# Each of the first 22 loads asked for only when the fourth load ahead of it has landed

## The chip, the cores and the metric

One core of a Trainium2 chip runs the kernel. The metric is device microseconds of one execution; a kernel's time is the median of its runs. TensorE was granted its full clock (1.0) throughout the profiled execution.

## What is computed

Linear attention with a quadratic feature map, and behind it a feed-forward layer on all 4352 tokens, in fp32:

```python
def phi(x):                       # r = 8: 64 features from 32 channels
    a = np.einsum('rd,bhsd->bhsr', S1, x)
    b = np.einsum('rd,bhsd->bhsr', S2, x)
    return np.einsum('bhsi,bhsj->bhsij', a, b).reshape(*x.shape[:-1], r * r)
q_p, k_p = phi(q), phi(k)         # batch 4, heads 4, 1088 positions
kv, z = einsum('bhsf,bhsd->bhfd', k_p, v), k_p.sum(2)
x = einsum('bhsf,bhfd->bhsd', q_p, kv) / (einsum('bhsf,bhf->bhs', q_p, z) + 1e-6)
h = x @ w_in                      # 4352 x 128 by 128 x 2048
out = (h * clip(h + 3, 0, 6) / 6) @ w_out
```

## The kernel before, in words

Tokens lie in the free dimension, channels on the partitions. The 4352 tokens are cut into eight chunks of 512 and one of 256 (`CHUNKS`); the 2048 hidden units into eight pairs of 128. For each chunk and pair TensorE makes `h` in three passes (high part of x by high and low part of the weights, low part of x by the high part), ACT and DVE make the gate, ACT and POOL or DVE split it into `gh` and `gl`, and TensorE adds it up into `o`.

The inputs arrive by DMA, all of it asked for by SyncE (SP). The keys come in eight groups (`k0` to `k7`, 256 or 320 KB), the values likewise (`v0` to `v7`, 264 or 330 KB), the queries by chunk (`q0` to `q8`, 256 KB), the two weight matrices in nine blocks (`wi0` and `wi1` with 256 KB, `wi2` to `wi4` and `wo0` to `wo3` with 512 KB). A weight block arrives as 64-bit words in a buffer `raw` and is turned into fp32 and split in two by seven steps: `scale` (L337) and `rest` (L340) on ACT, `sign` (L343) and `shift` (L347) on DVE, `word` (L351) on POOL, `high` (L354) on ACT, `low` (L357) on POOL or DVE.

The order of everything is written out by hand in `ORDER`, a list of names; each engine runs its own steps in that order. Each load is a step `ld_...` of SP (L322), put in by `load`, and has no needs but a free buffer. The loads stand in `ORDER` as k0, wi0, k1, wi1, q0, v0, v1, wi2, wo1, q1, k3, k2, wi3, v2, k5, v3, wi4, wo0, q3, q2, k4, wo2; before wo2, and only there, SP has another step to do, `move_1` (eight DMAs, L602). A small DMA of the projections (`sb_raw`, 80 KB, L288) goes ahead of them all and is not one of the loads that `load` makes.

What reads the early loads: `mm_k0` reads k0 (TensorE, L375), `scale_wi0` and `rest_wi0` read wi0, `rest_wi1` and `sign_wi1` read wi1, `mm_q0` reads q0, `kvt_0_...` (L405) read v0 and v1 together with the features of k0 and k1 (L385), `rest_wi2`, `sign_wi2` and `scale_wi2` read wi2. On ACT `rest_wi2` stands just ahead of `twice_0` (L439, L440), which copies out the sums of the first keys, and `scale_wi2` just behind it. On DVE `spread` (L427) and `shift_wi2` follow each other.

```python
def emit(_):
    nc.sync.dma_start(view(at(b)), place(name))

return plan.add(f"ld_{name}", SP, [], emit, [b]), b
```

Of the kernel before, what the change touches and what calls it, by code (L numbers as in the profile page):

```python
# [50 lines left out]
FAR = ((1,), (2, 3), (4, 5), (6, 7), (8,))  # L51

HALVED = 1
FIRST = 2


# [177 lines left out]
def fused_kernel(ctx: ExitStack, tc: tile.TileContext, inputs, places, outT):  # L234
    nc = tc.nc
# [17 lines left out]
    def at(buf):  # L253
        return room[buf.tag][buf.slot]
# [20 lines left out]
    def place(name):  # L275
        source, i, j = places[name]
        return inputs[source][i:j].rearrange("(p x) -> p x", p=P)
# [37 lines left out]
    s_done = plan.add("s_tr", PE, [s_done], s_tr, [st])  # L315
    s_done = plan.add("s_back", ACT, [s_done], s_back, [st])

    def load(tag, name, view):
        b = Buf((tag,))

        def emit(_):
            nc.sync.dma_start(view(at(b)), place(name))  # L322

        return plan.add(f"ld_{name}", SP, [], emit, [b]), b

# [2 lines left out]
    def weights(nm, hi, lo, j):  # L328
        name = f"{nm}{j}"
        i, k = BLOCKS[nm][j : j + 2]  # L330
        n = k - i
        hi, lo = hi[:, i:k], lo[:, i:k]
        ld, raw = load("raw", name, lambda t: t[:, :n])
        wb, rb, sb_ = Buf(("w",)), Buf(("r",)), Buf(ANY)

# [62 lines left out]
    def keys(b):  # L398
# [11 lines left out]
        for g in (2 * b, 2 * b + 1):  # L410
            t0, n = KGROUPS[g]
            lk, kb = load("kT", f"k{g}", lambda t, n=n: t[:, : n * P])
            lv, vb = load("v", f"v{g}", lambda t, n=n: t[:, :n, :].rearrange("p t x -> p (t x)"))
            parts, ab, ph = features(f"k{g}", n, "kph", lk, kb, ANY if b == 0 else ("a",), KEY_COLS[b])
            for t in range(n):
                i = t0 + t - b * KT
                prevs = plan.add(f"kvt_{b}_{i}", PE, [parts[t], lv, prevs], partial(kvt, n=n, t=t, i=i, ab=ab, ph=ph, val=vb), [ph, vb, sums, ab])
# [196 lines left out]
    def step(c, fp):  # L614
        c0, n = CHUNKS[c]
        hb, gb, gh, gl = (Buf((t,)) for t in ("h", "g", "gh", "gl"))
        ji, jo = (max(j for j, i in enumerate(BLOCKS[nm]) if i <= fp * 2 * P) for nm in ("wi", "wo"))
        halved = c < HALVED and fp < FIRST
        done = [None, None]
# [141 lines left out]
```

## Time and profile before

| what | us |
|---|---|
| median of 3 runs (228.47 to 229.22) | 228.91 |
| the profiled execution: its own time | 227.95 |
| span of the profiled execution, first to last instruction | 226.2 |
| TensorE busy | 219.7 (97% of the span) |
| ACT, DVE, POOL busy | 165.9, 163.1, 153.7 |

The profiled execution took 1.75 us more than its span, and 0.96 us less than the median. Times in the rows are counted from the first instruction. SP only issues DMAs; a row of SP's timeline is the time that the issue takes, and the DMA lands later by what the issue view gives.

### The profile page before, as it was taken

The numbers are of one execution on the slowest core, as the hardware profiler recorded it, in microseconds if no ns is written. First come the engines' busy times: TensorE is split into PE (matmuls) and PEld (weight loads), VectorE is DVE, ScalarE is ACT, GpSimd is POOL, SyncE is SP. The second block draws the span as 40 slices with busy tenths as digits, with TensorE's granted clock in tenths as the row PEclk, the third lists the DMA queues.
The fourth block names the chain that finished last, engine by engine and source line by source line (L and its number), as shares of the span: only waits on it lengthen the run. The fifth ranks groups of instructions, "written<-read, shape, count | busy, mean of one in ns | idle before, by whom it ended". The sixth has DMA issues, their size and how long they took to land.

```text
span 226.2 us, 4762 instructions
## 1 busy us (share of the span) xinstructions
PE 219.7 (97%) x1888; PEld 174.9 (77%) x1888; DVE 163.1 (72%) x216; ACT 165.9 (73%) x231; POOL 153.7 (68%) x111
## 2 busy tenths in 40 slices
PE   8789999999999999999999999999999999999994
PEld 3568768877788788777887888788888788888993
DVE  2799999999949889677866865686378644648561
ACT  4687997989785878656687865876686777785781
POOL 3859998998199734993899797356640498564471
PEclk9999999999999999999999999999999999999999
DMA  6997149233600001233001113020010000020010
GB/s 206 395 412 281 48 118 380 82 83 78 193 3 0 3 0 47 50 81 130 0 1 48 49 46 93 25 71 0 0 46 3 0 0 0 3 93 0 0 51 23
DMA packets 9430, 17.77 MB, mean 79 GB/s; under 512 B 1728, under 2 KB 2368, under 8 KB 9408
## 3 DMA queue, kind: packets, MB, share of 16 engines
q1 hardware_dynamic: 9408, 17.46, 23.2%
q8 instruction: 15, 0.25, 0.5%
q14 instruction: 7, 0.06, 0.1%
HBM read 11.30 MB, written 2.23 MB: 60 GB/s over the span
## 4 chain that ended last, share of the span: by engine, by line
PE 87%; DVE 5%; POOL 3%; DMA 1%; ACT 1%; issue 0%; SPq 0%; DVEq 0%
PE o L664 41%; PE h L627 14%; PE h L631 13%; PE h L628 13%; PE a L547 2%; DMA raw<-weights_dram 1%; DVE kph L385 1%; PE o L405 1%; PE a L542 1%; POOL gl L647 1%; DVE o L343 1%; POOL w L351 1%; DVE w L347 1%; PE a L375 1%; POOL wi_lo L357 1%; POOL kph L385 0%
## 5 line engine op out<-in xcount | busy, mean ns | idle before, releaser
L647 POOL TENSOR_TENSOR gl<-g,gh 128x1024 fp32r<-128x1024 f32 (+1 forms) x45 | 106.3, 2372 | 56.7 <-ACT gh L644 38.4
L641 DVE SCALAR_TENSOR_TENSOR g<-g,h 128x1024 f32<-128x1024 f32 (+1 forms) x72 | 82.8, 1153 | 35.4 <-ACT g L638 35.2
L638 ACT ACTIVATE g<-h 128x1024 f32<-128x1024 f32 (+1 forms) x72 | 70.7, 982 | 35.3 <-PE h L631 20.7
L644 ACT CAST gh<-g 128x1024 fp32r<-128x1024 f32 (+1 forms) x72 | 70.2, 1002 | 11.0 <-DVE g L641 6.0
L627 PE MATMUL h<-xh,wi_hi 128*128 128x512 f32 (+1 forms) x148 | 56.2, 381 | 0.0
L628 PE MATMUL h<-xh,wi_lo 128*128 128x512 f32 (+1 forms) x148 | 55.1, 373 | 0.0
L664 PE MATMUL o<-gh,wo_hi 128*128 128x512 f32 (+1 forms) x144 | 54.2, 379 | 0.0
L664 PE MATMUL o<-gh,wo_lo 128*128 128x512 f32 (+1 forms) x144 | 54.0, 378 | 0.0
L631 PE MATMUL h<-xh,wi_hi 128*128 128x512 f32 (+1 forms) x148 | 49.9, 374 | 0.0
L664 PE MATMUL o<-gl,wo_hi 128*128 128x512 f32 (+1 forms) x144 | 41.3, 380 | 0.1
L647 DVE TENSOR_TENSOR gl<-g,gh 128x1024 fp32r<-128x1024 f32 (+1 forms) x27 | 33.1, 1235 | 5.9 <-PE o L664 3.6
L627 PEld LDWEIGHTS h<-xh,wi_hi 128*128 128x128 f32 x148 | 27.8, 188 | 7.5 <-DVE g L641 1.2
L631 PEld LDWEIGHTS h<-xh,wi_hi 128*128 128x128 f32 x148 | 27.7, 188 | 5.5 <-DVE xh L470 0.2
L628 PEld LDWEIGHTS h<-xh,wi_lo 128*128 128x128 f32 x148 | 27.8, 188 | 4.6
L664 PEld LDWEIGHTS o<-gh,wo_hi 128*128 128x128 f32 x144 | 27.1, 188 | 5.3 <-issue 0.4
L664 PEld LDWEIGHTS o<-gh,wo_lo 128*128 128x128 f32 x144 | 27.1, 188 | 4.9
L664 PEld LDWEIGHTS o<-gl,wo_hi 128*128 128x128 f32 x144 | 26.0, 188 | 5.5 <-POOL gl L647 0.5
L590 POOL TENSOR_TENSOR qph<-ab 128x512 f32<-128x512 f32 (+1 forms) x16 | 16.1, 1018 | 0.2
L351 POOL TENSOR_TENSOR w<-w,r 128x512 int32<-128x512 int32 (+1 forms) x9 | 10.4, 1166 | 2.5 <-DVE w L347 2.0
L597 DVE STREAM_TRANSPOSE raw<-qph 128x512 f32<-128x512 f32 (+1 forms) x16 | 10.4, 665 | 1.9 <-POOL qph L590 1.9
L385 DVE TENSOR_TENSOR kph<-a,ab 128x512 f32<-128x512 f32 (+1 forms) x14 | 8.8, 635 | 0.5 <-ACT ab L378 0.5
L405 PE MATMUL o<-kph,v 128*32 128x64 f32 x288 | 6.2, 223 | 1.1 <-DVE kph L385 1.0
(104 smaller groups left out, 160.1 us busy)
## 6 DMA issues: line engine op xcount, KB each, us to landing
raw<-weights_dram SPq DMA_DIRECT2D x7, 512.0 KB, 6.3
phT<-raw SPq DMA_DIRECT2D x56, 64.0 KB, 2.0
qT<-tokens_dram SPq DMA_DIRECT2D x8, 256.0 KB, 6.0
outT_dram<-os SPq DMA_DIRECT2D x8, 256.0 KB, 2.2
v<-tokens_dram SPq DMA_DIRECT2D x4, 330.0 KB, 4.8
kT<-tokens_dram SPq DMA_DIRECT2D x4, 320.0 KB, 5.7
v<-tokens_dram SPq DMA_DIRECT2D x4, 264.0 KB, 6.1
kT<-tokens_dram SPq DMA_DIRECT2D x4, 256.0 KB, 5.7
```

What stands on the lines that cost most here:

```text
L351: nc.gpsimd.tensor_tensor(w, w, at(rb)[:, :n], op=ALU.add)
L385: engines[e].tensor_tensor(out, a_, b_, op=ALU.mult)
L590: engines[e].tensor_tensor(out, a_, b_, op=ALU.mult)
L597: nc.vector.transpose(turned_view()[:, :, r * half : (r + 1) * half].rearrange("p f (t w) -> p t f w", w=Q), src)
L627: nc.tensor.matmul(at(hb)[:, u, i:k], wi_hi[:, f], x, start=True, stop=False)
L628: nc.tensor.matmul(at(hb)[:, u, i:k], wi_lo[:, f], x, start=False, stop=False)
L631: nc.tensor.matmul(at(hb)[:, u, i:k], wi_hi[:, f], at(x_buf[c])[:, 1, i:k], start=False, stop=True)
L638: nc.scalar.activation(at(gb)[:, :, :n], at(hb)[:, :, :n], AF.Relu, bias=3.0, scale=1.0)
L641: nc.vector.scalar_tensor_tensor(at(gb)[:, :, :n], at(gb)[:, :, :n], 6.0, at(hb)[:, :, :n], op0=ALU.min, op1=ALU.mult)
L644: nc.scalar.copy(at(gh)[:, :, :n], at(gb)[:, :, :n])
L647: engines[e].tensor_tensor(at(gl)[:, :, :n], at(gb)[:, :, :n], at(gh)[:, :, :n].bitcast(F32), op=ALU.subtract)
L664: nc.tensor.matmul(at(ob)[:, :n], w, x[:, :n], start=left == acc["all"] and i == 0, stop=left == 1 and i == len(pairs) - 1)
```

## The change

Each call of `load`'s `emit` is kept in a list in the order in which SP issues them. From the fifth to the 22nd load an edge is added that makes the load wait for the landing of the load that stands four places ahead. The order of operations is as it was.

```diff
+AHEAD = 4
+FIRST_LOADS = 22
...
+    first = []
+
     def load(tag, name, view):
         b = Buf((tag,))
 
         def emit(_):
-            nc.sync.dma_start(view(at(b)), place(name))
+            i = nc.sync.dma_start(view(at(b)), place(name))
+            if AHEAD <= len(first) < FIRST_LOADS:
+                in_line = mybir.DependencyInfo(mybir.DependencyClass.Sync, mybir.DependencyReason.DATA)
+                tc.add_manual_dep(i.ins, first[-AHEAD].ins.name, in_line, reason="loads in line")
+            first.append(i)
```

## Rows read from the trace of the kernel before

**Rows 1.** The page's 40 slices of 5.655 us: TensorE's busy tenths, the DMA rate.

```profile
PE   8789999999999999999999999999999999999994
...
GB/s 206 395 412 281 48 118 380 82 83 78 193 3 0 3 0 47 50 81 130 0 1 48 49 46 93 25 71 0 0 46 3 0 0 0 3 93 0 0 51 23
```

**Rows 2.** Windows view, one stretch: its length, busy us by engine, clock, DMA.

```profile
17.40:226.00 208.60, 205.44 (x1596) 165.96 (x1589) 151.68 (x190) 154.29 (x201) 143.77 (x90) 1.00 0.18 57
```

**Rows 3.** Chain that ended last, up to 24 us: start, us, what.

```profile
1.64 3.09 DMA raw<-weights_dram
...
11.90 0.69 DVE w L347
```

**Rows 4.** SP's timeline: start, us, what is issued, count.

```profile
1.18 0.42 SPq L322 DMA_DIRECT2D kT<-tokens_dram  x1
...
2.59 0.43 SPq L322 DMA_DIRECT2D raw<-weights_dram  x1
3.06 0.43 SPq L322 DMA_DIRECT2D qT<-tokens_dram  x1
3.54 0.91 SPq L322 DMA_DIRECT2D v<-tokens_dram  x2
4.49 0.92 SPq L322 DMA_DIRECT2D raw<-weights_dram  x2
...
7.38 0.33 SPq L322 DMA_DIRECT2D raw<-weights_dram  x1
8.01 0.33 SPq L322 DMA_DIRECT2D v<-tokens_dram  x1
...
24.73 6.29 SPq L602 DMA_DIRECT2D phT<-raw  x8
```

**Rows 5.** Issue view, one issue each (sb k0 wi1 q0 v0 wi2 wi3 wo2 v6): KB, us to landing.

```profile
sb_raw<-weights_dram SPq DMA_DIRECT2D x1, 80.0 KB, 1.9
...
kT<-tokens_dram SPq DMA_DIRECT2D x1, 256.0 KB, 2.6
...
raw<-weights_dram SPq DMA_DIRECT2D x1, 256.0 KB, 4.1
...
qT<-tokens_dram SPq DMA_DIRECT2D x1, 256.0 KB, 4.2
...
v<-tokens_dram SPq DMA_DIRECT2D x1, 264.0 KB, 4.5
...
raw<-weights_dram SPq DMA_DIRECT2D x1, 512.0 KB, 5.6
...
raw<-weights_dram SPq DMA_DIRECT2D x1, 512.0 KB, 8.5
...
raw<-weights_dram SPq DMA_DIRECT2D x1, 512.0 KB, 3.7
...
v<-tokens_dram SPq DMA_DIRECT2D x1, 330.0 KB, 3.1
```

**Rows 6.** ACT's timeline: readers of wi1, wi2 and wi3; twice_0; in brackets idle before.

```profile
6.67 0.43 ACT L340 ACTIVATE r<-raw 128x256 int32<-128x256 uint32 x1 [0.72 <-DMA raw<-weights_dram]
...
10.19 0.70 ACT L340 ACTIVATE r<-raw 128x512 int32<-128x512 uint32 x1 [0.58 <-DMA raw<-weights_dram]
10.90 0.27 ACT L439 COPY kvt<-o 128x128 f32<-128x128 f32 x1
...
11.14 0.69 ACT L337 ACTIVATE w<-raw 128x512 f32<-128x512 f32 x1
...
17.86 0.68 ACT L337 ACTIVATE w<-raw 128x512 f32<-128x512 f32 x1
```

**Rows 7.** DVE's timeline: features of k1 and k0, spread, shift_wi2.

```profile
8.58 1.29 DVE L385 TENSOR_TENSOR kph<-a,ab 128x512 f32<-128x512 f32 x2 [0.50 <-ACT ab L378]
...
11.57 0.41 DVE L427 TENSOR_TENSOR z_diag<-mask,o 128x256 f32<-128x256 f32 x1
11.90 0.68 DVE L347 SCALAR_TENSOR_TENSOR w<-w,o 128x512 uint32<-128x512 uint32 x1
```

## The prediction, as made before the result was known

> **What bounds the kernel now.** I read the page's slices first. They fall into two parts [rows 1]: in the first three slices, up to 17 us, TensorE is not quite full and the DMAs run at about 400 GB/s (395 and 412 in the second and third slice); behind them TensorE is full to the last slice. The windows view says the same in one row: from 17.4 us to the end TensorE is busy 205.44 of 208.60 us [rows 2], and a bound of that kind cannot be moved by loads. So the change can act only on when this full stretch begins: what comes later there comes later at the end, one for one, since no idle time stands behind it in which to catch up.
>
> Next the chain of waits, for the first 24 us only [rows 3]. It holds one load, wi0 (asked for at 1.64, 3.09 us to landing). From there on it is engine work: ACT and POOL, then DVE from the features of k1 at 8.58 [rows 7] through `shift_wi2` at 11.90 to the low part of x, whereupon the full stretch of matmuls starts. No second load stands in it.
>
> Then SP's timeline and the issue view together, which give the landings (issue plus time to landing) [rows 4, 5]: k0 1.18 + 2.6 = 3.8; wi1 2.59 + 4.1 = 6.7; q0 3.06 + 4.2 = 7.3; v0 3.54 + 4.5 = 8.0; wi2 4.49 + 5.6 = 10.1; wi3 7.38 + 8.5 = 15.9. The same size takes the longer the later it is asked for: 256 KB take 2.6 us in an empty queue and 4.2 in a full one, and 512 KB rise from 5.6 to 8.5. That is a queue being drained at a steady rate, not a queue that lacks requests. The engines' timelines give who waits for a landing: ACT for wi1 (0.72 us, to 6.67) and for wi2 (0.58 us, to 10.19) [rows 6].
>
> **The change, part by part.** It adds 18 waits, one on each of the loads q0 to wo2, and removes or moves nothing.
>
> The instruction itself costs nothing that counts. SP already waits for landings: v2, the eighth DMA behind v0, is issued at 8.01, just as v0 has landed (8.0), and the issue takes 0.33 us [rows 4, 5]. I read this as a distance of eight that is in force already, and as the price of a wait: the issue follows the landing within hundredths of a microsecond. Behind a waiting load on SP stand only further loads until `move_1` at 24.73 [rows 4]; by then all of them are issued (below), so neither the moves nor the stores feel it.
>
> What counts is whether the transfer engines run dry between a landing and the first bytes of the load that was waiting for it. At that landing three loads are still in the queue. The smallest such three among the loads that something soon waits for are wi1, q0 and v0: 256 + 256 + 264 = 776 KB, which at the 400 GB/s of [rows 1] is 2.0 us of work. Against this stands the round trip, the part of the time to landing that is not transfer. For sb, in an empty queue, it is 1.9 us less 80 KB at 400 GB/s (0.2), so 1.7; for k0 2.6 - 0.65 = 1.95; for v6 3.1 - 0.85 = 2.3; for wo2 3.7 - 1.3 = 2.4 [rows 5]. The last three began in an idle queue, and wo2 and v6 beside the moves' DMAs, so they hold a slow start that a running queue need not show. The cover is 2.0 to 3 us, the round trip 1.7 to 2.4: just covered, or short by a few tenths now and then.
>
> The Trainium skill ("DMA: Bandwidth & Descriptors", section "Anatomy of one DMA") speaks against a wait of this kind: a DMA has a fixed cost of about 2.0 us, most of it receipt of the write, that no deeper work hides once one waits for its end, plus bytes over 436 GB/s. That figure is for the other issue path; with it wi2 would land 2.0 + 1.2 us after its issue at 6.67, at 9.9, before it lands now, and the sum would be zero. The rows give up to half a microsecond more, so their upper end is the harsher.
>
> Now load by load, taking for each the later of two times: its place in the queue as now, or its issue plus the time of its size in an empty queue [rows 5]. The first four, k0 to wi1, are issued as now, so wi0, the only load in the chain, lands where it did. q0 is asked for at 3.82 instead of 3.06 and could land at 3.82 + 2.6 = 6.4, before the 7.3 that its place gives: no change. v0 is asked for when wi0 lands, at 4.75, and with at most the 3.1 of v6 is there by 7.9, before its 8.0. v1 is asked for when k1 lands, which is before wi1 does (6.65), so it is there by 9.75 at the very latest; its matmuls also need features that DVE finishes at 8.58 + 1.29 = 9.87 [rows 7]. wi2 is the first that can slip: it is asked for when wi1 lands, 6.65, so at 6.67, and with 3.7 lands at 10.37 against 10.1, +0.27. With the 1.7 of sb plus 1.3 of transfer it would be 9.7, so its place decides and the slip is nothing.
>
> What would a late wi2 cost? ACT is idle before its first reader at 10.19, so that reader is late by the whole slip; `twice_0` at 10.90 and `scale_wi2` at 11.14 follow it back to back [rows 6], and `shift_wi2` on DVE, which is in the chain, needs the latter's end at 11.83 and starts at 11.90, as soon as `spread` lets it [rows 7]. The room is 0.1 us at most. So a slip of 0.27 puts at most 0.27 us on the end.
>
> The loads behind wi2 are hidden. wi3 lands at 15.9 and its first reader runs at 17.86 [rows 4 to 6]: 2 us of room, and the loads after it have more. Running the same rule on with the empty-queue times, the slip grows from 0.27 to about 0.5 at wi4, and the last load ahead of the moves, k4, is asked for at about 20, 4 us before `move_1`.
>
> Sum: between 0 and +0.27 us on the profiled 227.95. I take 0, since the full queue is nearer to a load that never meets an idle engine than to wo2 and v6, which did. Nothing below zero goes into the sum: the features at 8.58 waited 0.50 us for ACT's copy and not for a load, and an earlier wi2 finds DVE taken, since `spread` ends (11.57 + 0.41) only as `shift_wi2` starts [rows 7]. The median stands 0.96 us above the profiled execution; the change of 0 is put on the median.
>
> **The rivals.**
>
> *The round trip is not covered (slower).* The place is the landing of wi1 at 6.7 and the queue behind it. If each transfer engine that runs dry restarts as slowly as at the very beginning, a load costs more than the empty-queue times, say 0.5 us more: wi2 then lands at 10.87, ACT, `twice_0` and DVE shift by 0.77 less the 0.1 of room, and the time is 228.91 + 0.7 = 229.6. It decides from a landing of wi2 later than 10.2, and is over 0.3% (0.69 us, about what a measurement of this kernel can tell from no change) from 10.9 on. For it: the small gap between cover and round trip. Against it: three loads are in the queue at each landing, and the empty-queue times already contain one slow start.
>
> *Fewer transfers at a time land sooner (faster).* wi0 took 3.09 us where k0 took 2.6 for the same 256 KB [rows 3, 5]; if wi0 had lost these 0.5 us to the loads issued behind it, the chain would start 0.5 us sooner: 228.4. Against it: three of the loads behind it stay as they are, q0's bytes come after those of wi1, and the steady growth of the landing times says that the loads are served in turn. The Trainium skill ("DMA: Bandwidth & Descriptors", section "Latency and other measured facts") has a rule on its side, that a lighter load on HBM makes the fixed cost smaller; no row here shows it.
>
> *The change does nothing.* Both instructions are SP's, and an edge between two instructions of one queue could be taken as kept by their order, without a wait. q0 would be issued at 3.06 as now; the time is 228.9.
>
> **How the numbers follow.** The forecast (waits in force, wi2 late by 0 to 0.27): 0.79, 228.9, its own range 228.6 to 229.3 with the scatter of the runs. No wait: 0.08, 228.9. Round trip not covered: 0.08, 229.2 to 229.8, of which 0.05 lies over 0.3%. Sooner landings: 0.05, 228.1 to 228.5, of which 0.03 lies over 0.3%. So faster 0.03, same 0.92, slower 0.05. The range takes in the half microsecond that the faster rival gives and most of the slower one's: 228.4 to 229.5.
>
> **What would show it.** In the profile after, SP's timeline should have q0 issued at about 3.8, v0 at 4.75, wi2 at 6.7, and k4 near 19.5; the issue view should give times to landing of some 3 to 5 us instead of up to 8.5; ACT's reader of wi2 should start between 10.2 and 10.5, and the full stretch of TensorE at 17.4 to 17.7. The prediction is wrong if wi2's reader starts past 10.9, if wi0 lands before 4.3, or if `move_1` is issued later than now by more than the rest of the chain.

## The result, and the profile after

The changed kernel takes 230.6 us, the median of 11 runs (229.17 to 232.29); the kernel before takes 228.81 us in 11 runs on the same chips (227.99 to 229.23). The ratio is 1.009 with a 95% interval of 1.0061 to 1.0118: slower by 1.8 us. It lies outside the range and on the side that was given 0.05. The runs also differ in something that the profile before did not show: the granted clock of TensorE, averaged over the run, is 1.0 in two of the 11 runs (229.17 and 229.46 us), 0.993 in three (229.67 to 230.60) and 0.982 to 0.985 in six (230.23 to 232.29). Three runs of the kernels below (232.26 us with wi2 alone, 276.31 with distance five, 436.8 with three matmuls fewer) took over 1.5% longer than the fastest of their kernel and count neither in the ratios nor in the counts by clock.

The profiled execution of the changed kernel took 229.46 us with a span of 227.7 us, and is one of the two at full clock. It is 1.5 us longer than the profiled execution of before. The slices that answer to [rows 1] (TensorE's busy tenths, DMA rate):

```profile
PE   8869999999999999999999999999999999999994
...
GB/s 200 292 326 308 182 103 375 122 53 89 202 11 0 3 0 33 63 67 143 0 1 31 65 35 104 20 75 0 0 46 3 0 0 0 3 92 0 0 49 25
```

The rate in the second and third slice is 292 and 326 GB/s where it was 395 and 412, and the first loads go on into the fifth slice. The windows view shows the same in stretches of 2 us (length, busy us of PE, PEld, DVE, ACT and POOL with counts, granted clock, busy share of the DMA engines, GB/s), first before, then after:

```profile
6.00:8.00 2.00, 1.74 (x38) 1.27 (x37) 1.26 (x3) 0.94 (x3) 1.75 (x2) 1.00 1.05 394
8.00:10.00 2.00, 0.88 (x46) 0.76 (x48) 1.50 (x4) 1.22 (x4) 1.84 (x4) 1.00 1.03 416
10.00:12.00 2.00, 1.73 (x63) 1.40 (x63) 2.00 (x5) 1.80 (x5) 1.04 (x2) 1.00 1.03 400
```

```profile
6.00:8.00 2.00, 2.00 (x26) 0.99 (x26) 0.75 (x2) 0.90 (x4) 1.75 (x2) 1.00 0.84 282
8.00:10.00 2.00, 1.35 (x56) 1.15 (x56) 1.88 (x4) 1.24 (x4) 1.32 (x3) 1.00 0.97 318
10.00:12.00 2.00, 1.47 (x54) 1.18 (x54) 1.62 (x4) 0.38 (x2) 1.55 (x3) 1.00 0.92 279
...
19.00:227.50 208.50, 205.43 (x1593) 165.96 (x1589) 151.56 (x190) 154.31 (x201) 143.54 (x90) 1.00 0.19 60
```

The busy share of the DMA engines falls from 1.03 to 1.05 to as little as 0.84, although three or four loads are under way: that fits engines of which some have nothing to do at times. The last row answers to [rows 2]: the full stretch of TensorE is as dense as before (205.43 of 208.50 us), only it begins and ends 1.5 us later.

SP's timeline shows that the waits are in force (start, us, what is issued, count); it answers to [rows 4]:

```profile
2.58 0.43 SPq L328 DMA_DIRECT2D raw<-weights_dram  x1
3.85 0.33 SPq L328 DMA_DIRECT2D qT<-tokens_dram  x1
4.53 2.35 SPq L328 DMA_DIRECT2D v<-tokens_dram  x2
7.24 0.88 SPq L328 DMA_DIRECT2D raw<-weights_dram  x2
...
23.69 0.33 SPq L328 DMA_DIRECT2D kT<-tokens_dram  x1
26.30 0.59 SPq L612 DMA_DIRECT2D phT<-raw  x1
```

q0 is issued at 3.85 (forecast 3.8), v0 at 4.53, wi2 at 7.24 (6.7), k4 at 23.69 (19.5). The issue view for k1, wi1, v1, wi2 and wo1 (KB, us to landing) answers to [rows 5]:

```profile
kT<-tokens_dram SPq DMA_DIRECT2D x1, 320.0 KB, 4.4
...
raw<-weights_dram SPq DMA_DIRECT2D x1, 256.0 KB, 4.6
...
v<-tokens_dram SPq DMA_DIRECT2D x1, 330.0 KB, 3.5
...
raw<-weights_dram SPq DMA_DIRECT2D x1, 512.0 KB, 4.4
...
raw<-weights_dram SPq DMA_DIRECT2D x1, 512.0 KB, 5.6
```

wi2 lands at 7.24 + 4.4 = 11.65 instead of 10.10. ACT's timeline (in brackets idle before) shows what that does to its reader, to `twice_0` and to `scale_wi2`, which answers to [rows 6]:

```profile
11.74 0.67 ACT L350 ACTIVATE r<-raw 128x512 int32<-128x512 uint32 x1 [1.62 <-DMA raw<-weights_dram]
12.30 0.26 ACT L449 COPY kvt<-o 128x128 f32<-128x128 f32 x1
...
12.53 0.70 ACT L347 ACTIVATE w<-raw 128x512 f32<-128x512 f32 x1
```

The reader starts at 11.74 instead of 10.19, 1.55 us later, and the span is 1.5 us longer: one for one. The chain (start, us, what) now goes through two loads, wi1 and wi2, where [rows 3] had only wi0:

```profile
2.58 4.58 DMA raw<-weights_dram
...
7.24 4.41 DMA raw<-weights_dram
```

So between these two profiles the loss is the late landing of wi2. Whether the rest, up to the median, comes with the clock is tested below.

### The profile page after: what moved, and what is told of

It reads as the page before. It is cut to its first block, busy times and chain, and to the rows that moved or that the text cites. A ratio compares the mean times of both kernels' runs of the same rounds, so it can differ in the third digit from the quotient of the medians.

```text
span 227.7 us, 4762 instructions
## 1 busy us (share of the span) xinstructions
PE 220.9 (97%) x1888; PEld 175.5 (77%) x1888; DVE 163.5 (72%) x216; ACT 165.8 (73%) x231; POOL 153.7 (68%) x111
## 4 chain that ended last, share of the span: by engine, by line
PE 91%; DMA 4%; ACT 2%; SPq 1%; issue 1%; ACTq 0%
PE o L674 41%; PE h L637 15%; PE h L641 14%; PE h L638 14%; DMA raw<-weights_dram 4%; PE a L557 2%; PE o L415 2%; PE a L385 2%; PE a L552 1%; SPq L328 1%; PE o L552 1%; ACT w L347 0%; PE h L521 0%; ACT phT L503 0%; ACT r L350 0%
## 5 line engine op out<-in xcount | busy, mean ns | idle before, releaser
L350 ACT ACTIVATE r<-raw 128x512 int32<-128x512 uint32 (+1 forms) x9 | 5.7, 630 | 2.7 <-DMA raw<-weights_dram 2.7
```

## The experiments

All kernels were compared with runs of the kernel before on the same chip. Two theories were to be told apart from their rivals. *Dry queue*: with distance four the DMA engines run out of requests, v1 and wi2 land late, and the chain moves with wi2. *Clock*: the idle time that this leaves on TensorE before 15 us makes the granted clock fall in some executions, and that costs again.

| kernel | median us (runs) | ratio to before, 95% interval | runs with clock 0.997 or more: count, median us |
|---|---|---|---|
| before, all three comparisons | 228.7 to 228.8 (88) | | 81 of 88, 228.73 |
| the change, distance four | 230.6 (11) | 1.009 (1.0061 to 1.0118) | 2 of 11, 229.3 |
| distance eight | 228.79 (12) | 1.0012 (0.9989 to 1.0035) | 11 of 12, 228.68 |
| distance six | 228.68 (12) | 1.0002 (0.9991 to 1.0014) | 12 of 12, 228.68 |
| distance five | 229.05 (12) | 1.0013 (0.9991 to 1.0036) | 7 of 11, 228.71 |
| four, first five waits alone | 232.2 (5) | 1.016 (1.0144 to 1.0175) | 0 of 5 |
| four, later waits alone | 228.87 (12) | 1.0011 (0.9998 to 1.0024) | 11 of 12, 228.83 |
| four, wi2 alone | 229.18 (12) | 1.0031 (1.0003 to 1.006) | 7 of 11, 228.80 |
| four, v1 alone | 230.39 (6) | 1.0088 (1.0056 to 1.012) | 3 of 6, 230.24 |
| four, all but v1 | 230.04 (12) | 1.0063 (1.0036 to 1.009) | 3 of 12, 229.31 |
| four, TensorE's gaps filled | 230.0 (11) | 1.0047 (1.0022 to 1.0073) | 11 of 11, 230.0 |
| before, gaps filled | 228.98 (12) | 1.0015 (1.0 to 1.0031) | 12 of 12, 228.99 |
| before, three early matmuls fewer | 228.52 (12) | 0.9991 (0.9978 to 1.0004) | 9 of 11, 228.47 |
| before, 512 KB more ahead of v1 | 230.41 (8) | 1.0077 (1.0048 to 1.0106) | 4 of 8, 229.98 |

**Distance eight and six.** The edges stay, their reach is longer.

```diff
-AHEAD = 4
+AHEAD = 8        # the other kernel: 6
```

> Same edges, but each load waits for the eighth load ahead of it instead of the fourth; of the kernel before we read that about this distance is in force anyway. Theory 'dry queue' (with four, the transfer engines run out of requests between a landing and the first bytes of the load that waited for it): no loss, 228.8, reader of wi2 on ACT at 10.2. Rival 'the edge itself' (an added wait or changed semaphore costs time on SP whatever its distance): slower by the same 1.5 us as with four.

> Distance six. Theory 'dry queue': five loads (at least 3.4 us of work at 400 GB/s) stand behind each landing, so the loss is below 0.4 us, reader of wi2 before 10.6, DMA rate near 390 GB/s between 6 and 12 us. Rival 'every wait on a landing costs, since the slowest of the transfer engines tells when': about half of the loss, 0.7 us, would remain.

No loss that can be told in either: at most 0.35% with eight and 0.14% with six, by the upper ends of the intervals. So the edge itself is not what costs, and a distance of eight is what the kernel before has. With six the DMA rate between 8 and 12 us is that of before (windows view, same columns), after 349 GB/s between 6 and 8 us, where eight has 348:

```profile
8.00:10.00 2.00, 1.74 (x63) 1.26 (x59) 1.96 (x5) 1.34 (x4) 0.54 (x1) 1.00 1.04 416
10.00:12.00 2.00, 1.41 (x66) 1.16 (x56) 1.73 (x4) 1.27 (x4) 2.00 (x5) 1.00 1.01 387
```

One part of both expectations fell: ACT's reader of wi2 started at 10.90 with eight and 11.40 with six, not at 10.2 and before 10.6, since wi1 itself landed at 7.09 and 7.94 instead of 6.64. That belongs to the scatter of the first loads, below.

**Which waits.** First the head and the tail of the waiting loads, then single ones.

```diff
-FIRST_LOADS = 22
+FIRST_LOADS = 9
```

```diff
-            if AHEAD <= len(first) < FIRST_LOADS:
+            if 9 <= len(first) < FIRST_LOADS:
```

> Distance four, but on the first five of the waiting loads only (q0, v0, v1, wi2, wo1). Theory 'dry queue, through the landing of wi2': the whole of the loss is here, span 227.4 to 227.8, reader of wi2 on ACT at about 11.7, everything behind it late by 1.5 us. Rival 'the later loads': below 0.3 us.

> Distance four, but on the loads behind wo1 only (q1 to wo2). Theory 'dry queue, through the landing of wi2': these loads have 2 us of room and more, so nothing is lost: 228.8, span 226.2, though the DMA rate falls after 12 us. Rival 'the later loads': the whole 1.5 us. Theory on the clock (TensorE idles longer before 15 us and is granted less than its full clock in some executions, 0.98 to 1.0 in the runs of the changed kernel): clock 1.0 in all runs here, below 1.0 in some runs of the other one whose early loads wait.

The waits of q0 to wo1 carry the whole loss; their time is even above that of the changed kernel, and no run shows why. The later waits cost nothing that can be measured, although they drain the queue in the same manner, as the windows view of that kernel shows:

```profile
14.00:16.00 2.00, 1.70 (x36) 1.22 (x34) 1.83 (x5) 1.93 (x7) 1.52 (x2) 1.00 0.98 278
...
18.00:20.00 2.00, 2.00 (x59) 1.66 (x48) 1.89 (x5) 1.82 (x5) 2.00 (x3) 1.00 0.80 267
```

At 278 and 267 GB/s the loads behind wo1 still come in time: their room was real. The clock was not at 1.0 in every run of this kernel as expected: one of 12, the profiled one, has 0.992. The kernel with the early waits came with a profile at clock 0.984:

```profile
12.00:14.90 2.90, 1.61 (x17) 1.16 (x17) 2.11 (x4) 2.25 (x6) 0.29 (x1) 1.00 0.96 350
15.00:21.80 6.80, 6.08 (x120) 4.42 (x124) 4.93 (x14) 4.10 (x12) 4.07 (x4) 0.50 1.04 413
21.80:24.00 2.20, 2.20 (x27) 1.85 (x20) 2.17 (x6) 1.63 (x4) 1.36 (x2) 1.00 0.82 304
```

From 15.0 to 21.8 us TensorE was granted 0.50, the level of 1.2 GHz, after a stretch in which it was busy 1.61 of 2.90 us. wi2's reader is late by 2.16 us here (12.35 against 10.19, ACT's timeline), the span by 4.5 (230.7 against 226.2): some 2.3 us come behind that reader, in the stretch where the clock is down.

```profile
12.35 0.66 ACT L350 ACTIVATE r<-raw 128x512 int32<-128x512 uint32 x1 [1.83 <-DMA raw<-weights_dram]
```

```diff
-            if AHEAD <= len(first) < FIRST_LOADS:
+            if len(first) == 7:        # wi2 alone; the other kernel: 6, v1 alone
```

> One wait alone: wi2 for the landing of wi1, which holds back SP and so all later loads too. This is the wait on which the prediction put its whole sum. Theory 'one wait is covered by q0, v0 and v1 in the queue, the loss comes from several in a row': at most +0.3 us, 228.7 to 229.0, clock 1.0 in most runs. Rival 'a single drained queue is enough': 229.3 and more, clock below 1.0 in most runs.

> One wait alone: v1 for the landing of k1, which in the profiles so far lands anywhere from 5.5 to 7.3 us, hardly before wi1. Theory 'several in a row': below +0.3 us. Rival 'k1 lands so late that at its landing only about one load is left, the queue runs dry there, and all behind v1 is late': v1 lands at about 10, wi2 past 11.3, 229.3 to 230.6, the clock below 1.0 in some runs.

For wi2 alone the result lies between theory and rival (229.18 us). The runs fall in two groups: seven of 228.64 to 229.56 us at a clock of 0.999 or more, as before, and four of 230.50 to 231.03 at 0.993, besides the one of 232.26 at 0.985. For v1 alone the rival was right: the loss is that of the whole change (230.39 us). In its profile v1, issued at 6.42 when k1 had landed, took until 10.79, wi2 until 12.46, and ACT stood idle for it:

```profile
6.00:8.00 2.00, 1.26 (x25) 0.90 (x27) 0.81 (x2) 0.89 (x4) 1.76 (x2) 1.00 0.96 303
8.00:10.00 2.00, 1.31 (x56) 1.09 (x55) 1.81 (x4) 1.32 (x4) 1.39 (x3) 1.00 0.96 334
```

```profile
12.55 0.66 ACT L350 ACTIVATE r<-raw 128x512 int32<-128x512 uint32 x1 [2.50 <-DMA raw<-weights_dram]
```

Then two more kernels: one lets v1 go, the other sets the distance to five, which lets v1 wait for wi0.

```diff
-            if AHEAD <= len(first) < FIRST_LOADS:
+            if AHEAD <= len(first) < FIRST_LOADS and name != "v1":
```

> Distance four on all 22 loads but v1, which keeps the wait of before. Theory 'the wait of v1 for k1 does it, since k1 lands about as late as wi1': most of the loss goes, about what the wait of wi2 alone costs is left, 228.9 to 229.4. Rival 'any of the early waits drains the queue, v1 is only one of them': 230 and more.

```diff
-AHEAD = 4
+AHEAD = 5
```

> Distance five: v1 now waits for wi0 (landed at 4.5 to 4.9 in all profiles), wi2 for k1, wo1 for wi1. Theory 'cover at the landing of the late k1': v1 is not held back; wi2 is asked for at k1's landing, 5.5 to 7.3, with v1 still in the queue; loss between those of six and four, 0 to 0.4 us, 228.7 to 229.1. Rival 'number in flight alone': about half of the loss of four, 229.6.

Without v1's wait 1.3 us of the 1.8 are still there: v1's wait alone is enough for the loss, but most of it comes without that wait, and the theory that it is what does it falls. Not every early wait is enough by itself: wi2's alone cost nothing that can be told in the runs at full clock. With five nothing is left that can be told from no change, though the clock was 0.993 in four of 11 runs (229.79 to 230.17 us).

**A late load by another cause.** No wait is added; a load that nobody needs goes ahead of v1.

```diff
+            if name == "v1":
+                nc.sync.dma_start(room["g"][4].rearrange("p a x -> p (a x)"), inputs["tokens"][: P * 2 * CH].rearrange("(p x) -> p x", p=P))
             nc.sync.dma_start(view(at(b)), place(name))
```

> The kernel before, with no wait added, but one load of 512 KB more ahead of v1, into a buffer that nothing uses yet: v1, wi2 and all behind them land 1.25 us later, out of a queue that is full. Theory 'late v1 and wi2 are what costs, by whatever cause': +0.7 to +1.2 us at full clock and the clock below 1.0 in several runs, 229.5 to 231. Rival 'the waits on SP themselves': below +0.4 us.

1.6 us slower, out of a queue that is full (398 and 418 GB/s between 8 and 12 us). wi2 lands 2.26 us later than before, and ACT waits for it about as long as under the waits (1.62 us with the change, 2.50 with v1 alone):

```profile
12.45 0.67 ACT L342 ACTIVATE r<-raw 128x512 int32<-128x512 uint32 x1 [2.02 <-DMA raw<-weights_dram]
```

Four of its eight runs have a clock of 0.993 or less, and the other four a median of 229.98. So both parts of the loss follow from late loads without any added wait, and nothing in these runs asks for a further cost of the waits.

**The clock.** Seven matmuls of constants fill the gaps of TensorE; nothing reads what they write.

```diff
-... kvt_0_2 kvt_0_3 kvt_0_4 ...
+... kvt_0_2 kvt_0_3 fill fill fill kvt_0_4 ...
-... tr_0_0 sign_wi2:o ...
+... tr_0_0 fill fill fill fill sign_wi2:o ...
```

> The changed kernel with seven matmuls of constants more, whose results nothing reads, in the two gaps of TensorE that the late v1 and wi2 leave (three behind the fourth step on the first keys, four behind the first transposes). Theory on the clock (idle TensorE before 15 us is what takes the full clock away in 9 of the 11 runs of the changed kernel, and that is 1 to 2.5 us of its loss): clock 0.998 to 1.0 in nearly all runs, 229.2 to 229.5; the 0.6 us that the late wi2 costs at full clock stay. Rival 'late loads alone': as the changed kernel, 230.6.

> The same seven matmuls in the kernel before. Control: they fill time in which TensorE waits, clock 1.0 as without them, 228.6 to 228.9. Should they be faster or slower by themselves, the difference is to be taken off the run before.

The clock is 1.0 in all 11 runs, where the changed kernel had it in two. The time expected, 229.2 to 229.5 us, was missed: what remains is 230.0 - 228.98 = 1.0 us against the filled kernel before. That is the price of the late loads at full clock, more than the 0.6 that the two runs at full clock had made us expect. Of the 1.8 us in the median 0.6 to 1.3 are the clock's (230.6 less 230.0, or less the 229.3 of those two runs, if they are like the rest in all but the clock). Filling by itself does not pay: the filled kernel before is 0.2 us slower, with an interval that reaches down to 1.0.

```diff
-ld_wi0 scale_wi0 warm warm warm s_back ... ld_v0 warm mm_q0:h
+ld_wi0 scale_wi0 warm s_back ... ld_v0 mm_q0:h
```

> The kernel before, with no wait added, but without three of its matmuls of constants: two of the three that stand between the first keys and the copy of s_turn, and the one ahead of mm_q0. They compute nothing. Loads land as before. Theory on the clock (idle TensorE before 15 us takes the full clock away): below 1.0 in many runs, and in those 1 to 2.5 us slower, 230 to 231; runs at 1.0 as before. Rival 'the clock falls for another reason that comes with late loads': clock and time as before, 228.7.

This expectation failed: the clock hardly falls (0.990 at worst, at 228.76 us) and the time is that of before. In this kernel idle time before 10 us does not take the clock; its profile, then that of the one with the early waits, in stretches of 5 us:

```profile
5.00:10.00 5.00, 2.77 (x85) 2.05 (x80) 3.38 (x7) 3.33 (x10) 3.53 (x6) 1.00 1.02 383
10.00:15.00 5.00, 4.29 (x103) 3.43 (x103) 4.79 (x11) 4.35 (x11) 2.64 (x4) 1.00 1.02 401
```

```profile
5.00:10.00 5.00, 3.64 (x92) 2.37 (x86) 3.12 (x7) 2.65 (x9) 2.68 (x4) 1.00 0.89 299
10.00:15.00 5.00, 3.17 (x71) 2.34 (x71) 3.78 (x7) 2.87 (x8) 2.33 (x5) 1.00 0.93 295
```

TensorE idles more between 5 and 10 us in the first (2.77 us busy against 3.64) and keeps its clock; between 10 and 15 us it idles more in the second (3.17 against 4.29), and there the clock falls at 15. That idle time is the one that waits for wi2.

The clock can fall earlier, though. In the profile of the later waits alone TensorE waits for k1 from 5.80 to 7.27 us, and the clock is 0.50 from 7.3 to 10.7 (windows view, 2 us each):

```profile
6.00:8.00 2.00, 0.73 (x14) 0.73 (x16) 0.00 (x0) 0.03 (x1) 1.75 (x2) 0.83 0.97 322
8.00:10.00 2.00, 2.00 (x29) 1.45 (x25) 1.90 (x4) 1.38 (x4) 0.47 (x1) 0.50 1.05 419
10.00:12.00 2.00, 2.00 (x96) 1.80 (x93) 1.73 (x4) 1.20 (x3) 2.00 (x5) 0.82 1.04 401
```

Nor does any profile have the full clock from the start, though the first section says so of the profile before. In all 14 the first matmuls of constants stand 0.43 us apart, the later ones at full clock 0.22 us; the rows print 1.00 even so, and the mean clock leaves this stretch out. The traces have the clock rise at 3.9 to 9.9 us. Of the six profiles with a late wi2 (11.17 us or later) through early waits or the extra load, and without fillers, the four in which it rose by 4.75 us lost it again between 14.6 and 15.0; the two in which it rose later, at 6.68 (the change) and 9.85 (512 KB more), kept it. Six profiles show that these go together, not that one causes the other.

**What a late wi2 costs, profile by profile.** In seven profiles that kept the full clock and have no fillers (before, distance eight, six and five, three matmuls fewer, the change, 512 KB more) wi2 lands between 10.10 and 12.36 us, with waits or without. The time of the execution is in each of them that landing plus 217.7 to 217.9 us. The profile of the later waits alone (11.39 and 229.14 us) fits this too. Above it lie the profiles that lost the clock near 15 us: by 0.5 to 0.8 us where 0.50 lasted 3.4 us (wi2 alone, v1 alone, all but v1), by 2.3 us where it lasted 6.8 us (early waits alone).

## Why the prediction was wrong

*What bounds the kernel.* Right: the start of the full stretch decides, and a delay there reaches the end one for one (1.55 us at wi2's reader, 1.5 us at the end).

*The price of the wait, the distance of eight in force, the loads behind wo1, the moves.* Right: distance eight 1.0012, later waits 1.0011, both with 1 in the interval. `move_1` began 1.57 us later, with the rest of the chain (24.73 to 26.30). The sizes behind that were wrong, though: wi4 lands 4.25 us later (19.37 to 23.62), not about 0.5, and k4 is asked for at 23.69, not about 20. That these loads stay hidden is shown by the kernel whose later loads alone wait, not by the sum.

*The cover.* Wrong, and this is the step that failed. The prediction set 2.0 to 3 us of queued work against a round trip of 1.7 to 2.4 us and called it just covered, taking the three loads behind a landing as still to be moved. The rate says otherwise, 279 to 318 GB/s instead of 394 to 416. The trace after shows why they were not all still there. It holds sixteen signals for each load, as many as the core has DMA engines, and SP goes on after the last. Of k1's signals fifteen came from 5.14 to 5.83 us and the last at 6.53, whereupon v1 was issued at 6.55. By then fifteen of the sixteen of wi1 were in too. So for most engines only q0 and v0 were left, 520 KB or 1.3 us of work at 400 GB/s (an estimate), and the first signal of v1 came 2.2 us after its issue. Half of v0's signals were in at 7.47 us, as before (7.44); half of v1's at 9.06 instead of 8.46, half of wi2's at 10.55 instead of 9.74. That wi2 landed 1.55 us late and not 0.8 is again its last signals.

*The rule for wi2.* "The later of its place and its issue plus the empty-queue time" gave 10.37, called a bound; it landed at 11.65. v1, which was to be there by 9.75 "at the very latest", landed at 10.05. For wi2 both terms were too small. Its issue came at 7.24 and not 6.67, because wi1 landed at 7.16; and it took 4.4 us from there and not 3.7. Over the profiles, with the landings as issue plus time to landing:

| profile | k1 | wi1 | wi2 | wi1 to wi2 |
|---|---|---|---|---|
| before | 5.52 | 6.64 | 10.10 | 3.46 |
| distance eight / six / five | 5.99 / 7.31 / 5.93 | 7.09 / 7.94 / 6.57 | 10.81 / 11.32 / 10.21 | 3.72 / 3.38 / 3.64 |
| later waits alone; before, filled; before, fewer matmuls | 7.22 / 7.08 / 5.97 | 8.01 / 7.72 / 6.71 | 11.39 / 11.11 / 10.53 | 3.38 / 3.39 / 3.82 |
| the change | 6.53 | 7.16 | 11.65 | 4.49 |
| early waits alone; filled; all but v1 | 6.94 / 6.00 / 6.03 | 7.56 / 6.65 / 6.66 | 12.26 / 11.74 / 11.17 | 4.70 / 5.09 / 4.51 |
| wi2 alone; v1 alone | 6.86 / 6.41 | 8.05 / 7.09 | 12.08 / 12.46 | 4.03 / 5.37 |

Between the two landings lie 1362 KB (q0, v0, v1, wi2), 3.5 us at 400 GB/s. Kernels whose early loads do not wait at distance four take 3.4 to 3.8 us, those where one or more do 4.0 to 5.4. So the slip that was put at 0 to 0.27 us is 1.0 us for the change (4.49 less 3.46), to which come the 0.5 us by which wi1 landed later than before; over all pairs of the two groups it is 0.2 to 2.0.

*The scatter of the first loads* was not in the sum at all. k1 and wi1 are issued within 0.01 us of the same time in every kernel, and land anywhere from 5.5 to 7.3 and from 6.6 to 8.1. Half of k1's signals are in by 5.3 to 5.9 us in every profile; it is the last ones that scatter. The profile before showed both near the early end, and its 227.95 us lies below all 99 timed runs of that kernel (227.99 to 230.95). A margin of 0.3 us was read off one draw.

*The clock.* No term stood for it. The prediction took the clock of one profile for granted and priced idle time on TensorE as the delay alone.

*The rivals.* The uncovered round trip was the right mechanism in the right place: it named wi2's landing, the idle reader on ACT, and 10.9 as the point from which it is over 0.3%. Its price, 0.7 us, lies in the 0.6 to 1.5 that three comparisons give at full clock (the two runs, the filled kernels, the two profiles); it knew nothing of the clock's share, and its chance of 0.08 rested on the empty-queue times being bounds. Its own argument "three loads are in the queue" was the weak one. Sooner landings: wi0 landed at 4.51 in the profile after and at 4.5 to 5.0 elsewhere against 4.73, and the chain no longer ran through it. "Does nothing" is ruled out by SP's timeline. As for the fixed cost of about 2.0 us that the Trainium skill gives ("DMA: Bandwidth & Descriptors", section "Anatomy of one DMA"), with which wi2 was to land at 9.9: it took 4.4 us to land, of which 1.3 is transfer at 400 GB/s. Neither the figure nor the harsher rows described a load that is asked for behind a part-drained queue.

What stays open: how the early time splits between engines that have nothing queued and engines that restart slowly; why the last of the sixteen signals comes so late in some executions; and why the clock falls in some executions of one kernel and not in others.

## What to carry to other kernels

A wait for the landing of the n-th load ahead needs a cover well above the round trip of one load, since the last of sixteen signals ends the wait and most of the work counted as cover can be done by then: here four loads in flight (1.1 to 1.4 MB) lost a quarter of the rate or more, and six lost none that could be told. At the start of a kernel, take landing times from several profiles before reading a margin of tenths of a microsecond off them. And price a late load there twice: once as the delay of what waits for it, and once as idle time of TensorE ahead of its dense stretch, which can take its clock to half for several microseconds.

## What the runs showed of the hardware that was not expected

The granted clock fell to 0.50 at about 15 us for 6.8 us in the profile with the early waits, after 2.9 us in which TensorE had still been busy 1.61 us. With the later waits alone it fell at 7.3 us, after 1.47 us of waiting. In the kernel before the same is seen now and then: seven of 88 runs have a mean clock of 0.985 to 0.993, and take 229.2 to 231.0 us instead of 228.7.
